# Feed-forward items and the ranking product ahead of the cluster scores, ranking tables built in the prologue

## The chip, the cores and the metric

The kernel runs on one core of one Trainium2 chip. The metric is the device time of one execution in microseconds. Times inside the profile count from the first instruction of the profiled execution.

## The reference

```python
# attention: q, k, v are (4, 8, 768, 64); centroids (8, 16, 64)
q_assign = argmax(einsum('bhsd,hcd->bhsc', q_n, c_n))      # nearest of 16 centroids, rows normalised
k_assign = argmax(einsum('bhsd,hcd->bhsc', k_n, c_n))
mask = q_assign[:, :, :, None] == k_assign[:, :, None, :]
scores = where(mask, (q @ k^T) / sqrt(64), -1e9)
attn = softmax(scores)
x = (attn @ v) as (3072, 512)                              # all heads of a token side by side
# feed-forward: w_in is (512, 2048), w_out (2048, 512)
h = x @ w_in
out = (h * clip(h + 3, 0, 6) / 6) @ w_out
```

The arrays arrive as 64-bit floats; the kernel reads the weights as pairs of 32-bit words and turns them into 32-bit floats itself.

## The kernel before

**Tiles and stages.** The 32 heads are taken as 16 pairs. Pairs 0 to 6 are worked on with a full mask in a first stage; for pairs 7 (`FIRST`) to 15 tokens are ranked by cluster, scattered into sorted order, and only bands of the scores are made, in a second stage that starts at about 220 us. `SECOND` is pair 8. The ranking of pairs 7 and 8 is done during the first stage.

**The loop that orders the first stage.** The program order on each engine is written out by hand and engines work in that order. A loop runs over `n` in steps of two ("a double step"): `n` counts blocks of 128 keys against half of the queries, 12 to a pair, so `g, r = divmod(n, 12)` is the pair and the place in it. One double step issues, in this order:

- two times the scores (`scores`, L449, PE into `ps`), the exponentials (`exponentials`, L472, ACT, `ps` to `ex`, six buffers) and the sums over keys (`key_sums`, L480 and L483, mostly POOL, into `acc`);
- the product with the values of the double step before (`attn_v`, L493, PE into `pv`);
- at the end of a pair, the denominators (`sum_up`, L519, PE into `pd`, from `acc`);
- from n=42 on one or two scatters of pair 7's rows by indirect DMA on POOL's queue (`early_scatter`, L1277);
- then the lines that the change touches.

```python
early = decode[: share(n, r) - 1] if n < total and r == 4 else []
del decode[: len(early)]
for step in early:                 # decode steps of the weights, only where r == 4
    step()
if prep and r == 4:
    prep.pop(0)()                  # cluster_scores of the next pair
...                                # loads of later pairs (SP's queue)
if n in up_at:
    fill.pop(0)()                  # one feed-forward item: begin and end
    fill.pop(0)()
for step in prep:
    step()
for step in ranking.get(n, []):
    step()
...                                # the rest of the decode steps, then check_all
```

**Cluster scores and what follows.** `cluster_scores` multiplies a pair's turned queries and keys with the centroids (L386, PE into `pcs`) and transposes the product on DVE into a second PSUM tile, `pr` (L394). At r=6 `route` takes the maximum (`mx`, L400) and the comparison (`one_hot`, L406) from `pr` on DVE; at r=8 PE turns `one_hot` (`po`, L428) and ACT copies it to `xm`, the mask operand of the next pair's scores. For the pairs 7 and 8 `own_clusters` (L1105, L1111) stands in place of `route`.

**PSUM buffers.** In this stage `pcs`, `pr`, `po`, `pd`, the turns of queries and keys, the tiles of the ranking (`cnt`, `rk`) and the feed-forward tile `ph` all take turns in the two buffers of `psum_m`, in program order: each new tile takes the buffer of the one before the last, and waits for its last reader.

**Feed-forward items.** `up_at = (64, 68, 70, 72, 76, 80, 82, 84)` names the double steps in which an item `up(0, i)` of the first token block is issued; n=64 and n=76 are those with r=4, in which cluster scores are made too. An item is 16 matmuls from the token block `xb` (`ph`, L697), a lift on ACT (L564), a clip on DVE (L567) and, for odd i, sums on POOL (L729). The items of n=64, n=70 and n=76 begin with `kept_sums`: three subtractions of weights on DVE (`tx`, L625) and a store of `tx` to DRAM on SP's queue (L633). `xb` and its reciprocal denominators `rb` are loaded at the end of n=56 (L604, L608) and multiplied on DVE at the end of n=62 (`divide`, L557).

**Decode steps.** 32 chunks of weights are each loaded on SP's queue (`raw`, L263, three buffers; the load of chunk i+2 is issued in the first step of chunk i) and decoded in five DVE steps (L280, L286, L296, L302, L307), two of them with an operation on ACT (L276, L292).

**Ranking.** The dictionary `ranking` gives further steps by `n`: loads of pair 7's rows (`early_rows`, L1260 and L1269, SP's queue), `cluster_scores(FIRST)` at n=32, `own_clusters` at n=34, `count_up` (`cnt`, L1150, L1155) at n=36, and at n=40 `order_early` (the ranking product `rk`, L1167 to L1175, PE, then DVE) and `positions`, which writes `pos`, the rows of the scatters. `helpers` at n=30 builds the tables that these products read: 24 instructions on POOL (L967 to L995) into two tiles of which the names in the profile are `y`; five of them read `ident_q`, which DVE writes in the prologue (L1608). The prologue is the code ahead of the loop: identity matrices, the norm of the centroids, the turn and routing of pair 0.

Of the kernel before, what the change touches and what calls it, by code (L numbers as in the profile page):

```python
# [46 lines left out]
FIRST = NPAIR // 2 - 1  # L47
# [78 lines left out]
def fast_path(ctx, tc, ok, q, k, v, centroids, moe_w_in, moe_w_out, out):  # L126
# [65 lines left out]
    def scratch(shape, name, dtype=F32):  # L192

        if st["early"]:
            return psum_m.tile(shape, dtype, name=name, tag="m")
        return psum_t.tile(shape, dtype, name=name, tag="t")
# [19 lines left out]
    def turn_early(g, a):  # L216
        if a == 0 and g == FIRST:
            st["xf", g] = spare[:, 2 * NC2 * P : 3 * NC2 * P].rearrange("p (n c) -> p n c", n=NC2)
        elif a == 0:
            st["xf", g] = xp.tile([P, NC2, P], F32, name="xf")  # L220
        dst = st["xf", g][:, a * NCH : (a + 1) * NCH]
        nc.vector.transpose(out=dst.rearrange("p j c -> p (j c)"), in_=st["qk", g][:, a])
        if a == 1:
            st.pop(("qk", g))
# [35 lines left out]
    def load_weights(i):  # L260
        if i < len(chunks):
            st["raw", i] = rawp.tile([P, WC, 2], U32, name="raw")
            nc.sync.dma_start(st["raw", i], chunks[i][1])  # L263
# [68 lines left out]
    def idle(count):  # L332
        warm = psum_t.tile([P, 4, P], F32, name="warm", tag="t")
        for i in range(count):
            nc.tensor.transpose(out=warm[:, i % 4], in_=ident, identity=ident)
# [45 lines left out]
    def cluster_scores(g):  # L381
        c0, xf = (2 * g) % H * C, st["xf", g]
        ps = scratch([P, 512], "pcs")[:, 0 : NC2 * 2 * C]
        w = 2 * C
        for a in range(P // w):
            nc.tensor.matmul(  # L386
                ps[a * w : (a + 1) * w], lhsT=cnT[:, c0 : c0 + w], rhs=xf[:, :, a * w : (a + 1) * w],
                start=True, stop=True,
            )
        if st["early"]:  # L390
            cs = scratch([P, 512], "pr")[:, 0 : NC2 * 2 * C]
        else:
            cs = st["rankp"].tile([P, NC2 * 2 * C], F32, name="cs", tag="third")
        nc.vector.transpose(out=cs, in_=ps)  # L394
        st["cs", g] = cs
# [704 lines left out]
    def own_clusters(g):  # L1100
        st.pop(("xf", g))
        rankp = st.get("rankp", rtp)
        pr = st.pop(("cs", g)).rearrange("p (n c) -> p n c", c=C)
        mx = rankp.tile([P, 2 * NC2], F32, name="mx", tag="mx")
        nc.vector.reduce_max(out=mx, in_=pr, axis=AX.X)  # L1105
        shape = [P, 2, NCH, 2, C]
        if g <= SECOND:
            oh = st["oh", g] = smallp.tile(shape, BF16, name="oh", tag="sane")
        else:
            oh = st["oh", g] = rankp.tile(shape, BF16, name="oh")  # L1110
        nc.vector.tensor_tensor(  # L1111
            out=oh.rearrange("p a j t c -> p (a j t) c"), in0=pr,
            in1=mx.unsqueeze(2).to_broadcast([P, 2 * NC2, C]), op=ALU.is_ge,
        )
# [428 lines left out]
    up_at = (64, 68, 70, 72, 76, 80, 82, 84)  # L1543
    WRITING = (42, 84)

    def share(n, r):
        if n < 36:
            return {0: 4, 2: 4, 4: 4, 6: 1, 8: 4, 10: 4}[r]
        if n < 48:
            return {0: 4, 2: 4, 4: 2, 6: 2, 8: 5, 10: 5}[r]  # L1550
        if n < 60:
            return {0: 4, 2: 4, 4: 4, 6: 2, 8: 4, 10: 4}[r]
        if n < 72:
            return {0: 6, 2: 5, 4: 4, 6: 3, 8: 5, 10: 6}[r]
        return {0: 6, 2: 6, 4: 4, 6: 4, 8: 4, 10: 0}[r]

    def load_first(a):
        if a == 0:
            st["qk", FIRST] = spare[:, NC2 * P : 2 * NC2 * P].rearrange("p (a s) -> p a s", a=2)
        load_blocks(FIRST, a)  # L1560

    ranking = {
        10: [lambda: load_first(0)], 14: [lambda: load_first(1)],
        20: [lambda: turn_early(FIRST, 0)], 22: [lambda: turn_early(FIRST, 1)],
        30: [helpers], 32: [lambda: cluster_scores(FIRST)], 34: [lambda: own_clusters(FIRST)],
        36: [lambda: count_up(FIRST)], 40: [lambda: order_early(FIRST), lambda: positions(FIRST)],
    }
    for n, part in ((36, 0), (40, 1), (52, 2), (62, 3), (68, 4), (74, 5)):
# [14 lines left out]
    fill, checks = [], []  # L1583
# [13 lines left out]
    with tc.manual_schedule():  # L1597
        nc.scalar.dma_start(cen, centroids.rearrange("h c d -> (h c) d"))
        load(0, "q", "k")
        load(1, "q", "k")  # L1600
        constants()
        load(0, "v")
        load_weights(0)
        centroid_norm()
        for part in range(3):
            turn(0, part)
        idle(4)
        nc.vector.tensor_copy(out=ident_q, in_=ident)  # L1608
        load_weights(1)
        cluster_scores(0)  # L1610
        scores_qk(0)
        route(0)

        held = []
        turn(1, 0, values_bank())
        turn(1, 1, psum_t.tile([P, 4, P], F32, name="pqk", tag="t"), held)
        for part in range(2):
            route_turn(0, part)
        held.pop()()
        scores_qk(1)  # L1620

        for n in range(0, total + lag_d + 2, 2):
            g, r = divmod(n, per_pair)
            steps = [i for i in (n, n + 1) if i < total]
            prep = prep_items(g + 1, r)
            for i in steps:
                scores(i)
                exponentials(i)
                key_sums(i)
            for i in (n - lag_v, n - lag_v + 1):  # L1630
                if 0 <= i < total:
                    attn_v(i)
            m = n - lag_d + 1
            if m >= 0 and m % per_pair == per_pair - 1:
                sum_up(m // per_pair)
                ready(m)
            if WRITING[0] <= n < WRITING[1]:
                twice = n < 60 and n % NCH == 0
                for _ in range(2 if twice else 1):
                    if twice:  # L1640
                        pause()
                    writes.pop(0)()
            early = decode[: share(n, r) - 1] if n < total and r == 4 else []
            del decode[: len(early)]
            for step in early:
                step()
            if prep and r == 4:
                prep.pop(0)()
            if r == (4 if g == NKT else 6):
                load(g + 2, "q")  # L1650
                if g + 2 not in BLOCKS:
                    load(g + 2, "k")
            if r == 8:
                load(g + 1, "v")
                if g + 2 in BLOCKS:
                    load(g + 2, "k")
            if len(prep) > 1:
                prep.pop(0)()
            if n in up_at:
                fill.pop(0)()  # L1660
                fill.pop(0)()
            for step in prep:
# [3 lines that stand above are left out]
            if n < total:  # L1666
                rest = share(n, r) - len(early)
                for step in decode[:rest]:
                    step()
                del decode[:rest]  # L1670
            if r == 2 and "count" in st:
                st.pop("count")()
            check_all()
            checks.extend(later)
            later.clear()

        while checks or later:
            checks.extend(later)
            later.clear()
            check_all()  # L1680
        st["early"] = False
        st["moving"] = True
        open_late()
        fill.pop(0)()
        fill.pop(0)()
        held = []
        plan = late_plan()
        busy = {START[g] + at for g in range(SECOND, NPAIR) for at in st["full", g]}
        for i, point in enumerate(plan):
            if i == 3:  # L1690
                load_sums(1)
            elif i in (9, 11):
                st.pop("invert" if i == 9 else "complete")()
            held += point
            if not st["gating"]:
                for op, *args in held:
                    op(*args)
                held.clear()
            if fill and i not in busy:
                fill.pop(0)()  # L1700
        for op, *args in held:
            op(*args)
        st["last"] = True
        st["moving"] = False
        while fill:
            fill.pop(0)()
            if len(fill) == CHECK:
                flag = whether_good()
            elif len(fill) == HOLD:
                flag()  # L1710
# [363 lines left out]
```

## Time and profile before

| | |
|---|---|
| Median of 3 runs | 900.56 us (896.9, 900.56, 900.71) |
| The profiled execution | 902.71 us, its span 900.8 us |
| Mean granted TensorE clock | 0.991 |
| Busy: PE, DVE, ACT, POOL | 876.4, 583.3, 288.1, 596.8 us |
| Instructions | 17172 |

A row of the timeline gives start, duration, engine, line, operation, the tile written and the tiles read, shapes, the count of merged instructions, and in brackets how long the engine sat idle before it and on what. A row of the waits gives the waiting engine, tile and line, what it waited for, the total in us, the number of times, and the longest. A row of the windows gives the stretch, its length, the busy time and count of PE, weight loads, DVE, ACT and POOL, then the granted clock, the DMA share and GB/s.

### The profile page before, as it was taken

How to read it: one execution, taken by the hardware profiler on the slowest of the kernel's cores; microseconds unless marked ns; L12 is line 12 of the kernel's file. 1: busy time of each engine (PE TensorE's matmuls, PEld its weight loads, DVE VectorE, ACT ScalarE, POOL GpSimd, SP SyncE). 2: the span in 40 equal slices, each digit the busy share in tenths (PEclk: the TensorE clock that was granted, in tenths of full speed). 3: DMA queues.
4: the chain of work that ended last, by engine and by line, in shares of the span. 5: the costliest groups of instructions: out<-in, count | busy, mean ns of one | idle time of the engine just before them, and what ended most of it. 6: DMA issues, size and time to landing. Idle time of an engine off the chain costs nothing.

```text
span 900.8 us, 17172 instructions
## 1 busy us (share of the span) xinstructions
PE 876.4 (97%) x6031; PEld 692.6 (77%) x6031; DVE 583.3 (65%) x1340; ACT 288.1 (32%) x596; POOL 596.8 (66%) x1398
## 2 busy tenths in 40 slices
PE   9999997979999999999999999999999999999997
PEld 5443444637788798897897988988888889999996
DVE  6887887766879377485675765665664636447460
ACT  6887784642122213123031140220412302111120
POOL 3889897758868878778878787788787271212030
PEclk9999998989999999999999999999999999999999
DMA  7785695332987486586675856766636424233210
GB/s 205 149 224 141 174 246 152 118 109 58 222 226 186 98 215 164 144 201 165 151 197 133 197 160 152 185 148 152 169 109 160 114 65 124 75 90 94 76 36 28
DMA packets 262663, 130.90 MB, mean 145 GB/s; under 512 B 221132, under 2 KB 240104, under 8 KB 262568
## 3 DMA queue, kind: packets, MB, share of 16 engines
q1 hardware_dynamic: 238600, 81.22, 38.2%
q10 hardware_dynamic: 13600, 34.31, 13.4%
q0 software_dynamic: 10368, 14.18, 5.1%
q8 instruction: 50, 0.82, 0.4%
q14 instruction: 45, 0.37, 0.1%
HBM read 99.69 MB, written 29.97 MB: 144 GB/s over the span
## 4 chain that ended last, share of the span: by engine, by line
PE 88%; DVE 5%; DMA 3%; ACT 2%; issue 1%; POOL 1%; SPq 0%; POOLq 0%; DVEq 0%; ACTq 0%
PE Y L784 19%; PE uY L745 17%; PE X L784 13%; PE uX L745 13%; PE ps L449 5%; PE pv L493 4%; PE pv L1378 3%; PE ph L697 3%; PE ps L1321 3%; DMA rb<-rd 2%; PE pv L1321 1%; PE pcs L386 1%; PE pd L1402 1%; PE ps L1086 1%; ACT ex L472 1%
## 5 line engine op out<-in xcount | busy, mean ns | idle before, releaser
L1291 POOL DMA_INDIRECT xn<-xsd,pos x108 | 107.0, 990 | 44.5 <-DVE g_sb L756 15.1
L564 ACT ACTIVATE sx<-g_sb,half_c 128x512 f32<-128x512 f32 x88 | 63.6, 722 | 206.6 <-DVE g_sb L756 202.6
L1230 POOL MEMSET unread<- 128x1 f32 x918 | 97.5, 106 | 35.4
L1235 POOL DMA_INDIRECT kvd<-kvn,pos x96 | 96.7, 1007 | 21.3 <-issue 21.0
L483 POOL TENSOR_TENSOR acc<-acc,ex 128x768 f32<-128x768 f32 x56 | 102.8, 1836 | 10.9 <-ACT ex L472 7.9
L729 POOL TENSOR_TENSOR g_sb<-g_sb 128x256 f32<-128x256 f32 x48 | 34.0, 729 | 109.9 <-DVE g_sb L567 108.9
L1235 POOL DMA_INDIRECT qd<-qn,pos x84 | 89.6, 1066 | 16.6 <-issue 13.3
L745 PE MATMUL uX<-xb,w_in_sb 128*128 128x128 f32 x704 | 93.0, 275 | 0.0
L784 PE MATMUL X<-w_out_sb,g_sb 128*128 128x256 f32 x384 | 91.0, 382 | 0.3 <-DVE g_sb L567 0.3
L784 PE MATMUL Y<-w_out_sb,g_sb 128*128 128x256 f32 x384 | 89.0, 381 | 0.0
L784 PE MATMUL Y<-T,g_sb 128*128 128x256 f32 x384 | 88.7, 381 | 0.0
L745 PEld LDWEIGHTS uX<-xb,w_in_sb 128*128 128x128 f32 x704 | 85.7, 192 | 0.0
L784 PEld LDWEIGHTS X<-w_out_sb,g_sb 128*128 128x128 f32 x384 | 70.9, 190 | 14.0 <-issue 4.0
L784 PEld LDWEIGHTS Y<-w_out_sb,g_sb 128*128 128x128 f32 x384 | 72.0, 190 | 12.3 <-issue 2.3
L784 PEld LDWEIGHTS Y<-T,g_sb 128*128 128x128 f32 x384 | 72.2, 190 | 11.9 <-issue 2.1
L756 DVE TENSOR_TENSOR sx<-uX,sx 128x128 f32<-128x128 f32 x176 | 50.7, 288 | 33.4 <-ACT sx L763 30.3
L449 PE MATMUL ps<-xf 64*128 64x384 f32 x336 | 68.9, 487 | 0.9 <-ACT ex L472 0.9
L791 DVE TENSOR_TENSOR y<-y,Y 128x256 f32<-128x256 f32 x47 | 19.7, 420 | 75.9 <-PE Y L784 75.1
L756 DVE TENSOR_TENSOR g_sb<-uY,sx 128x128 f32<-128x128 f32 (+1 forms) x176 | 65.5, 413 | 0.0
L472 ACT ACTIVATE ex<-ps 128x768 f32<-128x768 f32 x84 | 63.8, 801 | 4.5 <-PE ps L449 4.3
L567 DVE SCALAR_TENSOR_TENSOR g_sb<-sx,g_sb 128x512 f32<-128x512 f32 x88 | 63.7, 726 | 2.0 <-ACT sx L564 2.0
L493 PE MATMUL pv<-ex,vt 128*64 128x384 f32 x336 | 63.5, 499 | 0.0
(239 smaller groups left out, 1691.8 us busy)
## 6 DMA issues: line engine op xcount, KB each, us to landing
tx<-td ACTq DMA_DIRECT2D x86, 384.0 KB
raw<-in_moe_w_in_dram SPq DMA_DIRECT2D x16, 512.0 KB
raw<-in_moe_w_out_dram SPq DMA_DIRECT2D x16, 512.0 KB
out_dram<-y SPq DMA_DIRECT2D x45, 128.0 KB
xb<-xd SPq DMA_DIRECT2D x11, 512.0 KB
piece<-qd SPq DMA_DIRECT2D x36, 96.0 KB
piece<-kvd SPq DMA_DIRECT2D x36, 96.0 KB
vs<-kvd SPq DMA_DIRECT2D x18, 192.0 KB
```

Source lines behind the costliest of these rows:

```text
L449: nc.tensor.matmul(st["ps", n][:, t, 0:HALF], lhsT=x[r, NCH + j], rhs=x[r, hf * NHC : (hf + 1) * NHC], start=first, stop=last, skip_group_ ...
L472: nc.scalar.activation(out=ex, in_=sc, func=ACT.Exp, scale=SM_SCALE)
L483: nc.gpsimd.tensor_tensor(out=acc, in0=acc, in1=ex, op=ALU.add)
L493: nc.tensor.matmul(pv[t * D : (t + 1) * D], lhsT=vt[:, t, j], rhs=ex[:, t], start=(j == 0), stop=(j == NCH - 1),)
L564: nc.scalar.activation(out=r, in_=h, func=ACT.Relu, bias=half_c, scale=1.0 / 6.0)
L567: nc.vector.scalar_tensor_tensor(out=g, in0=r, scalar=1.0, in1=h, op0=ALU.min, op1=ALU.mult)
L745: nc.tensor.matmul(dst, lhsT=w[:, kt], rhs=x(kt), start=(kt == 0), stop=(kt == HK - 1))
L756: nc.vector.tensor_tensor(out=out_, in0=in0, in1=in1, op=ALU.add)
L784: nc.tensor.matmul(bank[:, half * HC : (half + 1) * HC], lhsT=g_sb[:, kind, i], rhs=w[:, i], start=(first and i == 0), stop=(last and i == ...
L1230: nc.gpsimd.memset(unread, 0.0)
L1235: i = nc.gpsimd.indirect_dma_start(out=rows[name, g, t], in_=of(j), in_offset=None, out_offset=bass.IndirectOffsetOnAxis(ap=pos[:, a, j, t ...
L1291: nc.gpsimd.indirect_dma_start(out=xn[:, j, t], out_offset=None, in_=rows["xsd", g, t], in_offset=bass.IndirectOffsetOnAxis(ap=pos[:, 0, j ...
```

## The change

In double steps with r=4 (n=64 and n=76), the feed-forward item is issued ahead of the decode steps and of the cluster scores, where it came behind them. In double steps with r=4 the steps of `ranking` come ahead too: at n=40 `order_early`, `positions` and the load `early_rows(1)`, at n=52 the load `early_rows(2)`. `helpers` is issued in the prologue, after `ident_q` is written, and no longer at n=30. All other double steps keep their order.

```diff
     ranking = {
         10: [lambda: load_first(0)], 14: [lambda: load_first(1)],
         20: [lambda: turn_early(FIRST, 0)], 22: [lambda: turn_early(FIRST, 1)],
-        30: [helpers], 32: [lambda: cluster_scores(FIRST)], 34: [lambda: own_clusters(FIRST)],
+        32: [lambda: cluster_scores(FIRST)], 34: [lambda: own_clusters(FIRST)],
...
         nc.vector.tensor_copy(out=ident_q, in_=ident)
+        helpers()
         load_weights(1)
         cluster_scores(0)
...
+            if n in up_at and r == 4:
+                fill.pop(0)()
+                fill.pop(0)()
+            if r == 4:
+                for step in ranking.pop(n, []):
+                    step()
             early = decode[: share(n, r) - 1] if n < total and r == 4 else []
...
-            if n in up_at:
+            if n in up_at and r != 4:
                 fill.pop(0)()
                 fill.pop(0)()
```

## The prediction

> **What bounds the kernel now.** First the page's row of tenths for TensorE, then the waits of PE in three stretches (up to 140 us, 138 to 222 us, and the rest), then the timeline around the longest one.
>
> ```profile
> PE   9999997979999999999999999999999999999997
> ```
> ```profile
> PE pd L519 <- POOL acc L483: 1.0, 1, 1.0
> PE rk L1167 <- DVE pr L394: 0.8, 1, 0.8
> ```
> ```profile
> PE ph L697 <- DVE pr L394: 11.5, 2, 6.6
> ```
> ```profile
> PE ps L1321 <- DVE xsort L1064: 0.4, 1, 0.4
> ```
>
> PE is full in all but three slices of 22.5 us, and two of those hold the 11.5 us that it waits for DVE's transpose `pr`. Both waits stand in front of a feed-forward item (`ph`, L697). After 222 us the longest wait is 0.4 us, so PE alone sets the rest, and what PE gains ahead of it should reach the end. I therefore add up PE stalls.
>
> The timeline of PE, around the two items (n=64 and n=76):
>
> ```profile
> 139.09 0.85 PE L386 MATMUL pcs<-xf,cnT 128*32 128x384 f32 x8
> 144.83 6.54 PE L697 MATMUL ph<-xb,w_in_sb 128*128 128x256 f32 x16 [4.89 <-DVE pr L394]
> ...
> 157.63 0.51 PE L428 MATMUL po<-ident_q,one_hot 128*128 128x128 bf16 x6
> 157.97 3.67 PE L697 MATMUL ph<-xb,w_in_sb 128*128 128x256 f32 x16
> ...
> 182.74 0.85 PE L386 MATMUL pcs<-xf,cnT 128*32 128x384 f32 x8
> 190.20 6.05 PE L697 MATMUL ph<-xb,w_in_sb 128*128 128x256 f32 x16 [6.61 <-DVE pr L394]
> ...
> 202.50 3.72 PE L697 MATMUL ph<-xb,w_in_sb 128*128 128x256 f32 x16
> ```
> ```profile
> 145.00:147.00 2.00, 2.00 (x5) 1.63 (x6) 1.97 (x2) 0.00 (x0) 1.92 (x2) 0.50 0.35 137
> ```
>
> Why an item waits: `pcs` and `pr` take the two buffers of `psum_m`; `ph` needs the one that holds `pcs` until DVE has transposed it. Each wait is paid twice: after it the 16 matmuls take 6.54 and 6.05 us instead of 3.67, because the granted clock is 0.50 there (the windows row). So the two items lose 4.89 + 2.87 and 6.61 + 2.38, together 16.75 us. What makes `pr` late is DVE:
>
> ```profile
> 135.64 2.94 DVE L557 TENSOR_TENSOR xb<-xb,rb 128x1024 f32<-128x1024 f32 x1 [3.08 <-DMA rb<-rd]
> 138.51 0.68 DVE L302 SCALAR_TENSOR_TENSOR wwork<-raw,wwork 128x512 f32<-128x512 uint32 x1
> ...
> 143.59 0.69 DVE L280 TENSOR_SCALAR wwork<-raw 128x512 uint32<-128x512 uint32 x1
> 144.19 0.59 DVE L394 STREAM_TRANSPOSE pr<-pcs 128x384 f32<-128x384 f32 x1
> 144.69 1.78 DVE L625 TENSOR_TENSOR tx<-w_in_sb 128x256 f32<-128x256 f32 x1
> 146.50 2.37 DVE L625 TENSOR_TENSOR tx<-w_in_sb,tx 128x256 f32<-128x256 f32 x2
> 152.13 0.69 DVE L567 SCALAR_TENSOR_TENSOR g_sb<-g_sb,ph 128x512 f32<-128x512 f32 x1 [3.26 <-ACT g_sb L564]
> ...
> 153.33 0.56 DVE L400 TENSOR_REDUCE mx<-pr 128x24 f32<-128x384 f32 x1
> 153.93 0.62 DVE L406 TENSOR_TENSOR one_hot<-pr,mx 128x192 bf16<-128x192 f32 x2
> ...
> 171.08 0.69 DVE L280 TENSOR_SCALAR wwork<-raw 128x512 uint32<-128x512 uint32 x1
> ...
> 187.50 0.70 DVE L302 SCALAR_TENSOR_TENSOR wwork<-raw,wwork 128x512 f32<-128x512 uint32 x1
> ...
> 190.06 0.40 DVE L625 TENSOR_TENSOR tx<-w_in_sb 128x256 f32<-128x256 f32 x1
> 190.49 0.89 DVE L625 TENSOR_TENSOR tx<-w_in_sb,tx 128x256 f32<-128x256 f32 x2
> ```
>
> It waits 3.08 us for `rb`, divides, and does eight decode steps (138.51 to 143.59, one each 0.725 us) ahead of `pr`.
>
> **Part 1: the item ahead of the scores at n=64.** In the new order PE does `ph`, then `pcs`. `ph` needs `xb`, divided at 138.58, and a buffer whose last reader is long done; PE is there at 139.09. So `ph` runs 139.1 to 142.75, `pcs` to 143.6, and the next scores start 7.7 us before their old place (151.37, the end of `ph`). That is not all kept, for DVE now has more ahead of `pr` and of `one_hot`, for which PE's `po` waits two double steps' work later. DVE's order becomes: divide to 138.58; five decode steps of n=62 to 142.1; the three subtractions of `kept_sums` (L625), 1.78 + 2.37 = 4.15, to 146.3; the clip, whose lift is done by 143.5, to 147.0; three decode steps to 149.1; `pr` to 149.7; one step to 150.4; `mx` and `one_hot` to 151.7. PE needs 157.63 - 151.37 = 6.26 us from the end of this double step to `po`, so it is there at 149.9 and waits 1.8 us. Kept: 157.63 - 151.7 = 5.9 us. The subtractions are the unknown term, for the same three take 0.40 + 0.89 = 1.29 us at 190.06. The difference is what POOL does meanwhile:
>
> ```profile
> 144.36 3.77 POOL L483 TENSOR_TENSOR acc<-acc,ex 128x768 f32<-128x768 f32 x2
> ...
> 185.01 3.72 POOL L483 TENSOR_TENSOR acc<-acc,ex 128x768 f32<-128x768 f32 x2
> ```
>
> At 144.69 they run beside POOL's additions, at 190.06 beside nothing. I take 4.15, since POOL is as dense at the new place; with 1.29 nothing is left of the new wait (7.7 us kept), and if each of the three sat out one whole addition (1.88, half of 3.77) they would take 6.9 and 3.2 us would be kept.
>
> The Trainium skill, "SBUF — State Buffer", section "SBUF: two separate sides", states that DVE operations with two SBUF inputs and GpSimd operations hold one port pair exclusively, and that the loser fully blocks. By that rule three blocked subtractions are possible, and it speaks against putting them ahead of what PE waits for; the rows of 1.78 against 0.40 agree that there is such a price, and it makes the first rival.
>
> **Part 2: the same at n=76.** Everything starts 5.9 earlier. PE reaches the item at 182.74 - 5.9 = 176.8, `ph` ends at 180.5, `pcs` at 181.3, against 196.25 (190.20 + 6.05): 14.9 us ahead. DVE's twelve decode steps ahead of it end at 187.50 - 5.9 = 181.6. POOL's additions (185.01) are now at 179.1 to 182.8, so the subtractions lie half beside them; I take 2.5 us, between 1.29 and 4.15: 184.1; clip 184.8; three decode steps 187.0; `pr` 187.6. The next thing that needs this is `ph` of n=80, which now takes the buffer of `pcs`: PE is there at 181.3 + 6.25 (202.50 - 196.25) = 187.6. No wait worth a number; I put 0.2. So of 16.75 us about 14.7 are kept (14.9 with quick subtractions, 13.3 with 4.15). The ranking product of SECOND at n=82 is not moved.
>
> SP's queue: the store of `tx` waits for the subtractions and now stands ahead of a weight load.
>
> ```profile
> 142.90 0.33 SPq L263 DMA_DIRECT2D raw<-in_moe_w_out_dram  x1
> ...
> 148.90 0.33 SPq L633 DMA_DIRECT2D td<-tx  x1
> ```
>
> The load goes from 142.90 to about 146.5; the chunk is read two chunks later (171.08, then about 165), 18 us after: covered, and without that cover each late microsecond would stop DVE. ACT's lift moves ahead of one decode operation and nothing else: ACT waits there anyway.
>
> **Part 3: ranking steps at n=40 and n=52.** With `rk` ahead of the scores PE does not wait for `pr`: the 0.79 us below. DVE has the same instructions in another order. At n=52 two row loads come ahead of a weight load and of the loads of pair 6.
>
> ```profile
> 91.10 0.16 PE L1167 MATMUL rk<-y 128*128 128x2 bf16 x1 [0.79 <-DVE pr L394]
> ```
> ```profile
> 120.93 0.54 SPq L1269 DMA_DIRECT2D sx<-in_k_dram  x1
> 121.52 0.52 SPq L1269 DMA_DIRECT2D sx<-in_v_dram  x1
> ```
>
> Their issue is 0.54 + 0.52 = 1.06 us on SP; all loads behind are fetched a pair or two chunks ahead, and the store of `rd` still comes after the same loads. Nothing.
>
> **Part 4: tables in the prologue.** POOL's rows:
>
> ```profile
> 14.89 1.83 POOL L480 TENSOR_TENSOR acc<-ex 128x768 f32<-128x768 f32 x1 [12.10 <-ACT ex L472]
> ...
> 70.75 0.22 POOL L967 MEMSET y<- 128x128 bf16 x1
> ...
> 72.52 0.47 POOL L990 TENSOR_TENSOR y<-y,ident_q 32x160 bf16<-32x160 bf16 x1
> ...
> 77.57 0.41 POOL L995 COPY y<-y 128x64 bf16<-128x64 bf16 x2
> ```
> ```profile
> 8.49 0.22 DVE L1608 CAST ident_q<-ident 128x128 bf16<-128x128 f32 x1
> ```
> ```profile
> 83.64 0.83 PE L519 MATMUL pd<-acc,ones 128*32 128x384 f32 x2
> 85.52 0.85 PE L519 MATMUL pd<-acc,ones 128*32 128x384 f32 x6 [1.04 <-POOL acc L483]
> ```
>
> The tables take 7.2 us (70.75 to 77.98). In the prologue POOL is idle for 12.10 us until 14.89. It can do 1.8 us of them at once (70.75 to 72.52), must then wait for `ident_q` (8.71), and does the other 5.5 us to 14.2: hidden, with 0.7 us to spare; without it the first addition slips by what is over, and the six `ex` buffers take that up. DVE's short prologue operations beside it could sit out one such instruction, 0.47 us as L990; PE waits for several of them, so 0.5 is the far end, and I take 0. At the old place POOL's 7.2 us made `pd` late: it lasts from 83.64 to 86.37, 2.73 us, instead of 0.85. Without the tables the additions end well before, so 1.9 us go. What is late next there is DVE, which is not stopped by this.
>
> **The sum.** 1.9 + 0.8 in the first 95 us, 14.7 after: 17.4 us. The first 2.7 are kept only if `rb` (the 3.08 us wait) lands earlier by as much, since `xb` is ready only 0.5 us before PE wants it; it is issued behind PE's and DVE's progress, so I take them whole, and keep 0.5 as the other end. Span 900.8 - 17.4 = 883.4. The profiled execution took 902.71 (1.9 around the span); the median 900.56 lies 2.15 below it. From the median: 883.2 us. All good ends: 16.75 + 2.7 = 19.5, 881.1.
>
> **Rivals.** (a) The stall moves on along DVE. If each subtraction sits out an addition (6.9 us) and `rb` lands no earlier, `one_hot` comes at 154.4 and 3.2 us are kept at n=64; at n=76 the twelve steps end at 184.3, `pr` at 194.7 (6.9 + 0.7 + 2.2 + 0.6 later), PE wants it at 190.3 and waits 4.4 us: 7.8 us kept, 892.8 us. For it: DVE still has twelve decode steps and three subtractions ahead of `pr` at n=76. Against: it idles 3.26 us ahead of the clip (152.13) only because PE is late. The granted clock of 0.50 came after waits of 4.89 and 6.61 us; if it comes after 4.4 too, 2.4 more are lost, 895.2. The Trainium skill, "TensorE: Matmul & The Clock Gate", Part 1, gives an idle window of about 3.4 us for this; by that, the 1.8 us of my forecast cost no clock and the 4.4 would. Chance 0.20.
>
> (b) No change: DVE is the true bound from 138 to 222 and PE's gain is all spent waiting for it. Then DVE would hardly idle in this stretch; the 3.26 us ahead of one clip speak against it, and so does the walk above, in which DVE is ahead of PE again at n=80. 900 us, chance 0.07.
>
> (c) Slower: with `ph` first, PE itself stands behind the divide, with `pcs` and the scores behind it. Every microsecond that `rb` lands after 135.6 beyond 0.5 is then a stall of PE. It would have to land some 17 us later to eat the gain, by two row loads and a row buffer not yet free at n=52 holding SP up; at 21 us late, 904. Chance 0.05.
>
> **How the numbers follow.** The forecast has 0.68, (a) 0.20, (b) 0.07, (c) 0.05. About 0.5% (4.5 us) is what a measurement of this kernel can tell from no change. Forecast and (a) are faster by more, except the worst of (a): 0.87; same 0.08; slower 0.05. The range goes from all good ends less 2 us for the spread of runs, 879, to (a) at 892.
>
> **What would show it.** Right: no wait of `ph` for `pr`; all `ph` groups at 3.7 us and the granted clock at 1.00 throughout; `pd` at one piece of 0.85; a wait of `po` for `one_hot` below 3 us; tables done before 15 us. Wrong: a PE wait on `xb` or `one_hot` above 4 us, subtractions of 7 us, or new waits after 222 us.

## The result and the profile after

| | before | after |
|---|---|---|
| Median | 898.73 us of 4 runs (896.2 to 900.71) | 884.86 us of 4 runs (884.32 to 886.05) |
| The profiled execution, its span | 902.71, 900.8 us | 884.32, 882.5 us |
| Mean granted TensorE clock there | 0.991 | 0.998 |

The ratio of the times is 0.9849, with a 95% interval of 0.9815 to 0.9883; the medians differ by 13.9 us. The spans of the two profiled executions differ by 18.3 us. Why the two differences are not the same is the subject of the first experiment. Three executions that took far longer than all others of their kernel (909.66, 1485.06 and 2879.82 us) are left out of the medians and ratios below.

The page's row of tenths for TensorE, after:

```profile
PE   8999999999999999999999999999999999999997
```

The two thin slices with the waits are gone. The last slice, the end of the kernel, is as thin as before, and the first, the prologue, is thinner: there PE waits 1.1 us for the first loads and reaches the first cluster scores 0.12 us later than before. Waits of PE of the kernel after, from 60 to 222 us and then from 222 us to the end, the longest of each:

```profile
PE po L428 <- DVE one_hot L406: 1.2, 1, 1.2
...
PE uY L745 <- PE uX L745: 0.6, 1, 0.6
```

Of 11.5 us of waiting for `pr` nothing is left, and one new wait of 1.2 us stands in its place. The timeline of PE after, with both items, and below it three rows of the timeline before that the prediction did not need:

```profile
83.83 0.85 PE L519 MATMUL pd<-acc,ones 128*32 128x384 f32 x8
...
87.78 0.18 PE L1167 MATMUL rk<-y 128*128 128x2 bf16 x1
...
96.23 0.84 PE L428 MATMUL po<-ident_q,one_hot 128*128 128x128 bf16 x12
...
131.35 1.11 PE L519 MATMUL pd<-acc,ones 128*32 128x384 f32 x8
...
136.14 3.72 PE L697 MATMUL ph<-xb,w_in_sb 128*128 128x256 f32 x16
...
148.18 0.51 PE L428 MATMUL po<-ident_q,one_hot 128*128 128x128 bf16 x6 [1.21 <-DVE one_hot L406]
148.52 3.67 PE L697 MATMUL ph<-xb,w_in_sb 128*128 128x256 f32 x16
...
173.28 3.72 PE L697 MATMUL ph<-xb,w_in_sb 128*128 128x256 f32 x16
...
184.04 3.72 PE L697 MATMUL ph<-xb,w_in_sb 128*128 128x256 f32 x16
...
201.70 1.99 PE L784 MATMUL X<-w_out_sb,g_sb 128*128 128x256 f32 x8
```
```profile
98.65 0.84 PE L428 MATMUL po<-ident_q,one_hot 128*128 128x128 bf16 x12
...
133.78 1.63 PE L519 MATMUL pd<-acc,ones 128*32 128x384 f32 x8
...
220.16 1.99 PE L784 MATMUL X<-w_out_sb,g_sb 128*128 128x256 f32 x8
```

The double step of n=64 begins 2.95 us earlier (139.09 to 136.14). From there to the next item, that of n=68, takes 12.38 us (136.14 to 148.52) where it took 18.88 (139.09 to 157.97), 6.50 less. From the item of n=68 to that of n=76 nothing moves: 24.76 us (148.52 to 173.28) against 24.77 (157.97 to 182.74). From n=76 to n=80 it is 10.76 us (173.28 to 184.04) against 19.76 (182.74 to 202.50), 9.00 less. The sum, 18.5 us, is by how much `X`, the first product of the next part, comes earlier: 201.70 against 220.16. From there to the end of the span the two kernels take 680.8 and 680.6 us.

DVE's timeline after:

```profile
132.23 3.41 DVE L557 TENSOR_TENSOR xb<-xb,rb 128x1024 f32<-128x1024 f32 x1 [2.61 <-DMA rb<-rd]
...
139.06 1.47 DVE L625 TENSOR_TENSOR tx<-w_in_sb 128x256 f32<-128x256 f32 x1
140.57 2.96 DVE L625 TENSOR_TENSOR tx<-w_in_sb,tx 128x256 f32<-128x256 f32 x2
143.45 0.68 DVE L567 SCALAR_TENSOR_TENSOR g_sb<-g_sb,ph 128x512 f32<-128x512 f32 x1
...
147.76 0.62 DVE L406 TENSOR_TENSOR one_hot<-pr,mx 128x192 bf16<-128x192 f32 x2
...
177.95 1.61 DVE L625 TENSOR_TENSOR tx<-w_in_sb 128x256 f32<-128x256 f32 x1
179.59 0.89 DVE L625 TENSOR_TENSOR tx<-w_in_sb,tx 128x256 f32<-128x256 f32 x2
...
183.05 0.59 DVE L394 STREAM_TRANSPOSE pr<-pcs 128x384 f32<-128x384 f32 x1
```

The rows show the new order (subtractions and clip, then `one_hot`), the 4.43 us of the three subtractions at n=64 and the 2.50 at n=76, and `pr` of n=76 ready at 183.64, 0.4 us before PE asks at 184.04. POOL's timeline in the prologue, after:

```profile
14.03 0.41 POOL L995 COPY y<-y 128x64 bf16<-128x64 bf16 x2
15.01 1.82 POOL L480 TENSOR_TENSOR acc<-ex 128x768 f32<-128x768 f32 x1 [0.57 <-ACT ex L472]
```

The tables are done 0.57 us before the first addition can start.

### The profile page after: what moved, and what is told of

Its sections match the earlier page's. It is cut to its first block, busy times and chain, and to the rows that moved or that the text cites. A ratio compares the mean times of both kernels' runs of the same rounds, so it can differ in the third digit from the quotient of the medians.

```text
span 882.5 us, 17173 instructions
## 1 busy us (share of the span) xinstructions
PE 869.0 (98%) x6031; PEld 688.1 (78%) x6031; DVE 583.4 (66%) x1340; ACT 287.8 (33%) x596; POOL 596.3 (68%) x1398
## 3 DMA queue, kind: packets, MB, share of 16 engines
q10 hardware_dynamic: 13600, 34.31, 13.6%
## 4 chain that ended last, share of the span: by engine, by line
PE 91%; DVE 4%; DMA 2%; ACT 1%; issue 1%; SPq 0%; DVEq 0%; ACTq 0%
PE Y L784 19%; PE uY L745 17%; PE X L784 14%; PE uX L745 13%; PE ps L449 6%; PE pv L493 5%; PE pv L1378 3%; PE ph L697 3%; PE ps L1321 3%; PE pv L1321 1%; PE pcs L386 1%; DMA rb<-rd 1%; PE pd L1402 1%; PE ps L1086 1%; PE ps L1419 1%
```

## The experiments

**1. How far does the kernel before vary (before_again)?** No edit.

> The kernel before once more, to see whether its runs spread by more than those of the changed kernel (896.2 to 900.7 us against 884.3 to 886.1), and where. If the spread lies in the two waits of ph for pr and the slow matmuls behind them, this execution's profile shows them with another length (the first execution: 4.89 and 6.61 us of wait, 6.54 and 6.05 us for the 16 matmuls), its span differs from 900.8 us by about that much, and everything after the last item takes the same 681 us. Rival: the spread is spread over the whole execution, and the two items look as before.

Measured: on this chip, 903.78 us (898.89 to 906.71, 10 runs) and 904.16 for its own comparison (23 runs); profiled span 901.4 us. PE's item at n=64, a window row of it, and DVE's divide:

```profile
142.10 3.72 PE L697 MATMUL ph<-xb,w_in_sb 128*128 128x256 f32 x16 [1.96 <-DVE pr L394]
```
```profile
142.00:144.00 2.00, 1.90 (x9) 1.69 (x10) 1.97 (x3) 0.00 (x0) 1.85 (x2) 1.00 1.02 402
```
```profile
134.64 1.23 DVE L557 TENSOR_TENSOR xb<-xb,rb 128x1024 f32<-128x1024 f32 x1 [1.86 <-DMA rb<-rd]
```

Here `rb` is waited for 1.86 us instead of 3.08 and the divide takes 1.23 instead of 2.94, so `pr` makes PE wait 1.96 us instead of 4.89, and the clock stays at 1.00: the 16 matmuls take 3.72 instead of 6.54 us. That is 5.75 us less at n=64, and `X` comes 5.9 us earlier, at 214.25. The first profile of before was thus one of the long executions. Why the divide takes so much longer there shows in POOL's row of the first profile:

```profile
135.67 1.82 POOL L480 TENSOR_TENSOR acc<-ex 128x768 f32<-128x768 f32 x1
```

`rb` landed at 135.64, just as POOL began this addition, and the divide ended 1.09 us after the addition did. In before_again `rb` landed 1.0 us earlier, the divide was done at 135.87, and POOL's addition came only at 136.75. In ten of the thirteen profiles (that of items_only is not counted) the divide ends 1.08 to 1.10 us after an addition of POOL's; in the other three it takes 1.22 or 1.23 us. So one microsecond in a landing went with 2.7 us in the end of the divide, and so with the length of PE's wait and the clock behind it.

The other half of the expectation fell: the part behind `X` was not constant, 687.1 us here against 680.6. PE's waits from 222 us on show small stalls there that the first profile does not have:

```profile
PE uY L745 <- issue: 1.8, 3, 1.3
PE ps L1086 <- ACT bw L1357: 1.2, 1, 1.2
```

On this chip that part took 682 to 687 us in three profiled kernels, on the chip of experiment 8 it took 680.6 to 681.7 in all four. What makes the difference is open.

**2. The items alone (items_only, and items_again on another chip, beside the changed kernel).**

```diff
+            if n in up_at and r == 4:
+                fill.pop(0)()
+                fill.pop(0)()
             early = decode[: share(n, r) - 1] if n < total and r == 4 else []
...
-            if n in up_at:
+            if n in up_at and r != 4:
```

> The kernel before with the item moved ahead at n=64 and n=76, tables and ranking product left in place. My sum: 14.7 us of 17.4, a span near 886; no wait of ph for pr, po waits for one_hot by 1 to 2 us, the granted clock stays at 1.00. Rival (the moves need each other, since the tables' delay on POOL also delays DVE and the row scatters): clearly under 12 us. Rival (DVE is the bound): under 5 us.

> The kernel before with the item moved ahead at n=64 and n=76 alone, again, for an undisturbed profile and a time beside the changed kernel. If the 2.7 us of tables and ranking product reach the end, it is 2 to 3 us slower than the changed kernel; po at n=68 waits less for one_hot, since PE comes later. Rival: they are spent waiting for DVE's divide, whose rb is set by the transfers, and the two kernels take the same time within 1 us.

Measured: 890.7 us (4 runs) against 904.16 for the kernel before, ratio 0.985 (0.9817 to 0.9883); on the other chip 887.25 (6 runs) against 899.62, ratio 0.9864 (0.9837 to 0.9892), 12.4 us. The wait ahead of `po` in items_again is that of the whole change, not a shorter one as expected:

```profile
151.53 0.51 PE L428 MATMUL po<-ident_q,one_hot 128*128 128x128 bf16 x6 [1.21 <-DVE one_hot L406]
```

`X` stands at 205.06, 3.5 us behind that of the changed kernel on the same chip (201.59). The items are four fifths of the gain (ratios 0.9864 and 0.9831, experiment 8).

**3. The first item alone (item64_only).** As above, with `n == 64` and `n != 64` for the conditions on r. It asks whether the stall moves on along DVE to n=76, rival (a).

> The kernel before with the item moved ahead at n=64 alone. My sum: 5.9 us kept there, and the wait at n=76 stays at about 6.6 us with 2.4 us of slow matmuls, a span near 895. Rival (the stall moves on along DVE): the wait at n=76 grows by what n=64 saved, and the span stays at 900.

Measured: one run of 898.53 us, span 896.7. PE's timeline:

```profile
138.36 3.72 PE L697 MATMUL ph<-xb,w_in_sb 128*128 128x256 f32 x16
...
181.69 5.47 PE L697 MATMUL ph<-xb,w_in_sb 128*128 128x256 f32 x16 [6.61 <-DVE pr L394]
```

The wait at n=76 is 6.61 us, to the hundredth what it was: DVE is there as much earlier as PE. The stall of n=64 does not move on to n=76, as rival (a) has it.

At n=64 this execution kept more than the 5.9 us expected: 11.11 us to the next item (138.36 to 149.47) against 18.88, so 7.8. PE does not wait for `one_hot` at all, although the subtractions took 4.96 us, because here the divide was done at 134.86, 3.5 us before PE came. In the changed kernel it was done 0.5 us before. The new wait of 1.2 us thus hangs on the divide as much as on the subtractions.

**4. How much of the loss is the clock (warm_before)?** The old order, with 30 and 42 turns of the identity behind the cluster scores of n=64 and n=76 to keep PE busy while it waits.

```diff
+        for _ in range({6: 30, 8: 42}.get(g, 0) if st["early"] else 0):
+            nc.tensor.transpose(out=whole_ps[:, NC2 * 2 * C :], in_=ident, identity=ident)
```

> The kernel before with the order unchanged, but PE does 30 and 42 more transposes of the identity (0.15 us each, into unused columns of the tile that holds the cluster scores) after the scores of n=64 and n=76, so that it is busy while it waits for pr. This splits the stall into wait and clock. If the slow matmuls come from the idle time ahead of them, ph takes 3.7 us both times, the granted clock stays at 1.00, and the span falls by about 5.25 us (2.87 + 2.38) to 895.5 with ph starting where it did. Rival: the matmuls are slow because their weights or xb are in use by DVE at that time: ph still takes over 6 us and the time is the same.

Measured: 900.93 us (12 runs) against 904.16, ratio 0.9965 (0.9947 to 0.9983), 3.2 us. PE's timeline, and one row of the windows:

```profile
139.99 3.49 PE L392 MATMUL pcs<-ident 128*128 128x128 f32 x30
144.96 3.72 PE L700 MATMUL ph<-xb,w_in_sb 128*128 128x256 f32 x16 [1.48 <-DVE pr L397]
...
187.51 5.41 PE L700 MATMUL ph<-xb,w_in_sb 128*128 128x256 f32 x16 [1.88 <-DVE pr L397]
```
```profile
189.00:191.00 2.00, 2.00 (x6) 1.55 (x6) 0.00 (x0) 0.00 (x0) 0.00 (x0) 0.50 0.73 233
```

The turns took 0.116 us each, less than planned, and left gaps. At n=64 the item starts where it did (144.96 against 144.83) and runs at full clock; at n=76 it is still slow, after an idle gap of only 1.88 us. So the run recovers n=64's clock alone and does not price the clock of both. That a share of the loss is the clock's stands (3.2 us, with the item of n=64 starting no earlier), and the expectation's rival falls: DVE works on the weights at n=64 here too, and the matmuls are fast.

**5. Tables alone, ranking alone (tables_only, ranking_only), and both (early_both).** `helpers()` moved to the prologue; or `ranking.pop(n, [])` ahead in steps with r=4; or both, items left in place.

> The kernel before with the tables built in the prologue alone. My sum: pd at n=38 in one piece (1.9 us), nothing lost in the prologue, and of these 1.9 us the wait of ph for pr at n=64 takes back what rb does not land earlier: a span of 899 to 900.8. Rival (the stall at n=64 hides anything gained ahead of it): pd is mended, but PE gets to the end of n=76 at the same time as before.

> The kernel before with the ranking steps of n=40 and n=52 moved ahead alone. My sum: the wait of rk for pr (0.79 us) goes; span 0 to 0.8 us shorter. Rival: early_rows(2) ahead of the weight load and of pair 6's loads holds SP up, rb lands later, and the divide of n=62 starts later than 135.6 us.

> The kernel before with tables and ranking steps moved, items in their old place. Tables alone moved a 1.9 us stall of pd into the wait of rk for pr (0.79 to 2.44 us), the ranking steps alone took 0.8 us; together they should take 2.7 us between pd of n=38 and po of n=44 (15.0 us before, 12.4 in the changed kernel). Of it the wait at n=64 may swallow all, so the span is 898 to 901 on the scale of the first profile. Rival: the sum of the two alone, 0.8 to 1 us.

Measured: tables alone 904.66 us and ranking alone 902.72 (one run each, the kernel before 902.37 there, with runs from 898.21 to 907.75, so these two times decide nothing and the rows have to); both 897.25 (10 runs) against 899.62 on the chip of experiment 8, ratio 0.9975 (0.9951 to 0.9999), some 2.3 us and barely clear of the noise. Where the tables' gain went, in PE's timeline and windows of tables_only:

```profile
84.53 0.85 PE L519 MATMUL pd<-acc,ones 128*32 128x384 f32 x8
...
91.77 0.16 PE L1167 MATMUL rk<-y 128*128 128x2 bf16 x1 [2.44 <-DVE pr L394]
```
```profile
94.00:96.00 2.00, 2.00 (x10) 1.10 (x6) 1.40 (x4) 0.81 (x1) 0.83 (x1) 0.50 1.32 236
```

`pd` is whole, as forecast, but PE then waits for DVE's `pr` ahead of `rk`, 2.44 us instead of 0.79: of 1.88 won, 1.65 is given back at the next wait, and behind it the clock falls to 0.50, which was not expected. From `pd` to `po` it takes 16.4 us (84.53 to 100.91) where before takes 15.0 (83.64 to 98.65); 15.0 - 1.88 + 1.65 would be 14.8, so the slow clock costs about 1.6. Ranking alone takes 14.25 (83.16 to 97.41), and both together 12.4 (83.98 to 96.38), the same as the whole change. The ranking product's move is what lets the tables' move through. In early_both PE then waits at n=64 as in experiment 1, and its matmuls stay fast:

```profile
139.05 3.72 PE L697 MATMUL ph<-xb,w_in_sb 128*128 128x256 f32 x16 [1.79 <-DVE pr L394]
```

Its profiled span, 893.9 us, is below what was expected for that reason: the expectation reckoned from the long execution.

**6. The subtractions behind the cluster scores (sums_late).** The changed kernel with `kept_sums` of n=64 and n=76 issued after `prep.pop(0)()`.

```diff
-                        kept_sums(sooner[u], nc.vector)
+                        st["subtract"] = lambda: kept_sums(sooner[u], nc.vector)   # u in (0, 4)
...
             if prep and r == 4:
                 prep.pop(0)()
+            if "subtract" in st:
+                st.pop("subtract")()
```

> The changed kernel with the three subtractions of n=64 and n=76 put behind the cluster scores again (item ahead, its weight subtractions not). If the wait of po for one_hot (1.2 us in the changed kernel) comes from DVE's 4.4 us of subtractions ahead of pr, it goes, and the span falls by about 1.2 us to 881.3; no other wait appears. Rival: the wait is for the divide and the decode steps, and stays over 0.8 us.

Measured: 889.9 us (6 runs) against 902.37 for the kernel before, ratio 0.986 (0.9825 to 0.9895). The expectation failed. DVE's timeline, PE's, and a window:

```profile
141.66 0.69 DVE L567 SCALAR_TENSOR_TENSOR g_sb<-g_sb,ph 128x512 f32<-128x512 f32 x1 [4.02 <-ACT g_sb L564]
...
144.81 1.06 DVE L625 TENSOR_TENSOR tx<-w_in_sb 128x256 f32<-128x256 f32 x1
145.91 2.97 DVE L625 TENSOR_TENSOR tx<-w_in_sb,tx 128x256 f32<-128x256 f32 x2
...
149.97 0.62 DVE L406 TENSOR_TENSOR one_hot<-pr,mx 128x192 bf16<-128x192 f32 x2
```
```profile
150.39 0.77 PE L428 MATMUL po<-ident_q,one_hot 128*128 128x128 bf16 x6 [2.38 <-DVE one_hot L406]
150.95 5.13 PE L700 MATMUL ph<-xb,w_in_sb 128*128 128x256 f32 x16
```
```profile
151.00:153.00 2.00, 2.00 (x7) 1.64 (x6) 1.58 (x3) 0.81 (x1) 1.92 (x2) 0.50 0.98 166
```

PE does not wait for `pr`; it waits for `one_hot`, and the subtractions still stand ahead of that. Worse, DVE now idles 4.02 us ahead of the clip, a hole that the subtractions filled before, so `one_hot` comes later, PE waits 2.38 us and its clock falls. From the item of n=64 to `X` it takes 68.4 us (137.18 to 205.59) where the changed kernel took 65.6 (136.14 to 201.70).

**7. `xb` and `rb` loaded two double steps later (rb_late).** The changed kernel; it tries rival (c).

```diff
-            later.append(lambda: later.append(lambda wait=invert(): later.append(wait)))
+            later.append(lambda: later.append(lambda wait=invert(): later.append(lambda: later.append(lambda: later.append(wait)))))
```

> The changed kernel with the loads of xb and rb issued two double steps later (at the end of n=60 in place of n=56, some 8 us). It tries the price of my third rival: PE now stands behind the divide, with cluster scores and scores behind it. If so, ph of n=64 waits for xb by about the delay of rb less 0.5 us (6 to 8 us), the clock falls to 0.50 behind it, and the span grows by the wait and up to 2.9 us more: 889 to 893. Rival: DVE's decode steps run in the time and little is lost, under 2 us.

Measured: 891.64 us (4 runs) against 902.37 for the kernel before, ratio 0.9867 (0.9822 to 0.9912). DVE's and PE's timeline:

```profile
137.29 2.70 DVE L557 TENSOR_TENSOR xb<-xb,rb 128x1024 f32<-128x1024 f32 x1 [6.22 <-DMA rb<-rd]
```
```profile
140.13 6.75 PE L697 MATMUL ph<-xb,w_in_sb 128*128 128x256 f32 x16 [4.39 <-DVE xb L557]
```

PE stands behind the divide for 4.39 us, less than the 6 to 8 expected, since `rb`, issued 6.9 us later, landed 5.1 us later (137.29 against 132.23). Then it runs 16 matmuls in 6.75 us; the wait of `po` disappears in it, and `X` comes 5.7 us late, at 207.44. Rival (c)'s mechanism is real; `rb` was simply not late in the changed kernel.

**8. The changed kernel once more, and the subtractions behind `one_hot` (after_again, sums_after_route).** The second as in 6, but the `st.pop("subtract")()` stands behind the steps of r=6, where `route` issues `one_hot`.

```diff
             for step in ranking.get(n, []):
                 step()
+            if r == 6 and "subtract" in st:
+                st.pop("subtract")()
```

> The changed kernel once more, beside the one with the items alone and two variants, so that all share the runs of the kernel before. Ratio to before 0.985 as on record (13 to 14 us); its runs lie closer together than those of before, since the waits whose length changed from execution to execution are gone. Rival: the gain on record was a matter of one chip and is under 10 us here.

> The changed kernel with the three subtractions of n=64 and n=76 put behind the reading of pr (behind route at n=66 and own_clusters at n=78), where nothing that PE waits for stands behind them for 5 us. From the changed kernel's rows: the clip ends at 141.2, pr at 143.9, one_hot at 145.8 us, PE wants it at 147.0: the wait of 1.2 us goes, and 0.5 to 1.2 us of the time. Rival, as when they stood behind the scores: DVE idles ahead of the clip and pays the subtractions afterwards, and another wait of PE (on one_hot, the clip or rk) takes the place, with the clock falling behind it: same or slower.

Measured: the changed kernel 884.17 us (883.45 to 884.66, 5 runs) against 899.62 (896.22 to 902.91, 16 runs), ratio 0.9831 (0.98 to 0.9861), with the same wait of 1.22 us ahead of `po` and, as expected, its runs much closer together; the other 882.81 us (882.35 to 884.62, 6 runs), ratio 0.9815 (0.9789 to 0.9842). PE's and DVE's timeline of sums_after_route:

```profile
148.64 0.51 PE L428 MATMUL po<-ident_q,one_hot 128*128 128x128 bf16 x6
```
```profile
142.36 0.69 DVE L567 SCALAR_TENSOR_TENSOR g_sb<-g_sb,ph 128x512 f32<-128x512 f32 x1 [4.38 <-ACT g_sb L564]
...
146.67 0.62 DVE L406 TENSOR_TENSOR one_hot<-pr,mx 128x192 bf16<-128x192 f32 x2
147.21 0.42 DVE L625 TENSOR_TENSOR tx<-w_in_sb 128x256 f32<-128x256 f32 x1
147.66 3.05 DVE L625 TENSOR_TENSOR tx<-w_in_sb,tx 128x256 f32<-128x256 f32 x2
```

No wait is left ahead of `po`. In its profiled execution the first loads landed later than in after_again, so the stretches are compared: from `pd` to `X` 116.58 us (85.58 to 202.16) against 117.90 (83.69 to 201.59), 1.3 us less, about the 1.22 us that PE waited. The divide was early here too, done 3.4 us before PE came (134.48, `ph` at 137.88), but that is not why the wait went: DVE idles 4.38 us ahead of the clip, and a divide 2.9 us later would only have shortened this idle time. The medians differ by 1.4 us, and the runs of the two overlap in one. It is the fastest version here, by little.

## Why the prediction was right

The predicted 883.2 us stand against 884.86; faster was right, and in the main for the reasons given. That the time came out within 1.7 us is in part luck, as the sum below shows. By its steps:

- **Part 1.** Kept 6.50 us at n=64, where 5.9 were forecast. The new wait ahead of `po` is 1.21 us, not 1.8. The subtractions took 4.43 us, close to the 4.15 taken, and the divide ended 0.50 us before PE came, where the forecast had 0.51. What was sized too high is the chain behind the subtractions: from the clip to `po` the forecast adds up 5.4 us (146.3 to 151.7), and it took 4.7 (143.45 to 148.18). Several of these DVE operations start 0.1 us before the one ahead has ended, and `po` starts before both halves of `one_hot` are done (148.18 against 147.76 + 0.62). The 0.50 us did not come as the forecast has it, by `rb` landing as much earlier as PE. `rb` landed 3.4 us earlier (132.23 against 135.64), but POOL's addition held the divide, as in experiment 1, until 1.09 us after its own end (134.55):

```profile
132.73 1.82 POOL L480 TENSOR_TENSOR acc<-ex 128x768 f32<-128x768 f32 x1
```

- **Part 2.** 9.00 us at n=76, where 14.7 - 5.9 = 8.8 were forecast; subtractions 2.50, as taken. `ph` of n=80 finds `pr` done with 0.4 us to spare, so the 0.2 put for it was nothing.
- **Part 3.** `rk` runs without a wait. The edits on SP's queue cost nothing: among DVE's waits from 96 to 222 us none is for a weight load.
- **Part 4.** Tables end about 14.4 us, 0.57 to spare (forecast 14.2, 0.7); `pd` 0.85 in one piece. Behind both parts PE is 2.42 us earlier at `po` (98.65 to 96.23) and 2.95 at n=64; the half microsecond more is the next denominators, which also shorten, 1.63 to 1.11. Forecast: 2.7. The step that was incomplete is the sentence that DVE, next in line there, "is not stopped by this". It is what PE waits for next: alone, the tables' 1.9 us are lost again at `rk` and in the slow clock behind it (experiment 5). The sum came out because both parts were made, not because each is worth its term.
- **The sum against the span: 17.4 forecast, 18.3 measured. Against the median: 13.9.** The sum was taken from the first profile of before, and that was one of its long executions, with 4.89 us of wait and 2.87 us of slow clock at n=64; another has 1.96 and none (experiment 1). Of the 4.5 us between span and median, 4.0 are the profiled execution of before (902.71) lying above its median and 0.5 that of after lying below. On the chip of experiment 8 the runs of before fall into two groups: seven of 896.2 to 897.8 us at a mean clock of 0.994 to 0.995 and seven of 901.3 to 902.9 at 0.991 to 0.992, with two between. Groups 5 us apart fit n=64 with and without the slow clock, but no execution of before in the lower group was profiled: argued, not shown. The changed kernel's 884.17 us are 12 to 13.6 below the one and 17.1 to 18.7 below the other. Against the medians the gain was forecast too high by 3.5 us. The time came out only 1.7 us too low because the median of three runs that it was taken from, 900.56, lies 1.8 above that of the four: that is luck.
- **The rivals.** (a) falls by experiment 3, by the 1.21 us wait, and because its subtractions of 6.9 us were nowhere seen. (b) falls with the result. (c) is a true mechanism whose condition did not come about (experiment 7).
- **The clock.** The forecast wait of 1.8 us was priced without a slow clock, and at the 1.21 us that came the clock stayed at 1.00. The Trainium skill, "TensorE: Matmul & The Clock Gate", Part 1, gives an idle window of about 3.4 us for a drop. That length does not agree with the runs: 1.88 us (experiment 4), 2.38 (6) and 2.44 (5) were enough for 0.50. At 1.8 us the missing price would have been a matter of luck: 1.5 us more, if it went as in experiment 6.
- **The port.** The Trainium skill, "SBUF — State Buffer", section "SBUF: two separate sides", states that a DVE operation with two SBUF inputs and an operation of GpSimd that reads SBUF shut each other out, for the whole length of the one that began first. The traces agree. The divide waits an addition of POOL's out (experiment 1). The same three subtractions took 1.29 us beside nothing, 4.43 at n=64, 2.50 at n=76, 3.47 (0.42 + 3.05) in experiment 8 and 4.96 in experiment 3, by what POOL did beside them, and never the 6.9 of rival (a). DVE's decode steps, which have no two inputs in SBUF (`wwork` is a PSUM tile), took 0.65 to 0.73 us up to 225 us in all thirteen profiles, beside POOL's additions or not.

## What to carry to other kernels

On an engine that works in program order, issue work whose inputs are ready ahead of a tile whose buffer a late engine must give back; and put what nobody waits for (here the subtractions) behind the operation that another engine waits for, not merely behind an earlier one. A gain is worth what the next wait lets through: run the parts alone and together, for of two parts here one alone lost 1.4 us between `pd` and `po` and the other gained 0.8, and together they gained 2.6. And sum against more than one profiled execution of the kernel before when a DMA's landing sits inside the stall that is to be removed: here a landing 1.0 us earlier went with a stall 5.75 us shorter.

## What the runs showed of the hardware that was not expected

The granted clock of TensorE fell to 0.50 with idle gaps of 1.88, 2.38, 2.44, 4.39, 4.77, 4.89 and 6.61 us, and stayed at 1.00 with gaps of 1.21, 1.48, 1.79 and 1.96. A gap of 1.88 that does and one of 1.96 that does not mean that length alone does not decide; what does is open. Nor is it decided when a gap ends: in warm_before the matmuls resume at 187.51, the clock is still 1.00 up to 188, and it falls within the next microsecond:

```profile
188.00:189.00 1.00, 1.00 (x4) 0.83 (x4) 0.65 (x2) 0.00 (x0) 0.00 (x0) 0.61 0.01 0
```

With the clock at 0.50 the 16 matmuls of an item took 5.1 to 6.75 us instead of 3.67 to 3.72. A wait of 1.9 to 2.4 us can therefore cost 1.5 to 1.7 us more than its own length, as in warm_before at n=76 (5.41 us instead of 3.72) and in sums_late (5.13 instead of 3.67).
